# RWKV-7 recurrence and squared-ReLU feed-forward: the third channel tile of the first layer filled with zero rows from 64 to 128

## The chip, the cores and the metric

The kernel runs on one core of a Trainium2 chip. The metric is the device time of one execution in microseconds (us). In the profile PE is TensorE's matmul side and PEld its weight-load side, DVE is VectorE, ACT is ScalarE, POOL is GpSimd and SP is SyncE.

## The reference

For each of 4 batches and 8 heads a 40x40 state runs over 768 time steps. Its outputs of all heads form 3072 tokens of 320 channels, which go through a feed-forward network with 2048 hidden units:

```
for t in range(S):
    y[:, :, t] = einsum('bhd,bhde->bhe', rt, state)
    Sa = einsum('bhde,bhe->bhd', state, at)
    state = state * wt[:, :, None, :] - einsum('bhd,bhe->bhde', Sa, bt) + einsum('bhd,bhe->bhde', vt, kt)
x = y.transpose(0, 2, 1, 3).reshape(3072, 320)
h = maximum(x @ w_in, 0)        # w_in: 320 x 2048
out = (h * h) @ w_out           # w_out: 2048 x 320
```

## The kernel before

The recurrence is computed in chunks of 128 time steps: 6 chunks for each of 4 batches, 24 in all, in the order chunk 0 of all batches, chunk 1 of all batches, and so on. For each chunk `decay` and `rest` transpose the inputs, form running products of the decays and the products of keys with keys by head; `inverse` builds the inverse of a triangular 128x128 matrix for every head, in 6 levels of three stages (a transposition, a product that leaves PSUM through a mask, a product that is added); `chain` does what depends on the state. Heads lie in pairs, 64 partitions each, of which 40 hold data. So most matmuls contract over 128 rows, and those of `products` (the tiles `aT,bT`, `aT,kT`, `rT,vT`, `rT,xnT`) over 40 rows, one parity of heads on partitions 0 to 39 and the other on 64 to 103.

`gather` turns the outputs of two chunks into a tile `tokens`, 256 tokens by channel. The 320 channels are cut into three channel tiles, `KT`: rows 0 to 127, 128 to 255, and 256 to 319, the third with 64 rows only. `w_in` lies in SBUF in the same three channel tiles. For each of 16 hidden tiles (`f`) the first layer makes three matmuls into one PSUM bank, one for each channel tile; this is called an f step below. ACT then takes the ReLU (L395) and DVE the square (L396). The second layer contracts over the 16 hidden tiles, 128 rows each (`w_out,hid`). There are 12 pairs of chunks, hence 12 x 16 = 192 f steps. A float32 matmul of this program is two weight loads and two matmul instructions in the profile, so an f step has six of each: four over 128 rows, two over 64.

The engines take the work in the order in which the generators at the end of the kernel yield it: between two stages of `inverse` or `decay` of the next chunk stand a stage of the present chunk's `chain`, one of `rest`, and up to one part of the feed-forward network of earlier chunks (`second`). A scheduler in the framework may then reorder instructions of one engine.

`mm`, at L65, is the helper that records nearly all matmuls, so they share that line; they are told apart by their tiles (`out<-moving, stationary` or the reverse: the program's names of what is read and written).

Of the kernel before, what the change touches and what calls it, by code (L numbers as in the profile page):

```python
# [17 lines left out]
def kernel(  # L18
# [9 lines left out]
    moe_w_out: bass.AP,  # L28
    out: bass.AP,
):  # L30
    # The recurrence runs in chunks of C steps.  Within a chunk, with E_j the product of the decays
    # of the steps before j and all products taken relative to the middle of the chunk:
    #   a' = a E_t, k' = k / E_t+1, b' = b / E_t+1           (per key channel)
    #   N = strictly lower (a' b'^T), A = strictly lower (a' k'^T)
    #   x = (I + N)^-1 (a' S^T + A v)                         (the rows S a of all steps)
    #   y = E_t (r S + low(r v^T) k' - low(r x^T) b')
    #   S <- E_C (S + v^T k' - x^T b')
    # (I + N)^-1 is exact: the inverses of its diagonal blocks, doubled in size level by level.
    # Heads go in pairs, 64 partitions or columns each; tiles by head are [., parity, pair, .].
    nc = tc.nc  # L40
    B, H, S, D = r.shape
    DM = H * D
# [29 lines left out]
    pair = lambda t_, q: t_[:, 2 * q:2 * q + 2, :].rearrange("t h d -> t (h d)")  # L72
    over4 = lambda m_: m_.unsqueeze(1).to_broadcast([128, NP, 128])

# [1 line left out]
    class Ring:  # L76
        def __init__(self, name, n, shape, fill, pads):
            self.tiles = [single(f"{name}{i}", shape) for i in range(n)]
# [17 lines left out]
    def load(i):  # L96
        bb, c = order[i]
        loaded[i] = {}
        for nm, ring in rings.items():
# [2 lines left out]

    load(0)

# [1 line left out]
    ident = single("ident", [128, 128])  # L106
    make_identity(nc, ident)
    ones = single("ones", [128, MID])
# [2 lines left out]
    nc.gpsimd.memset(upper, 1.0)  # L111
    nc.gpsimd.affine_select(out=upper, in_=upper, compare_op=Alu.is_gt, fill=0.0, base=0,
                            pattern=[[1, 128]], channel_multiplier=-1)
    # -1 at [2p, 2p + 1]: the first level, transposed.
    first = single("first", [128, 128])
    nc.gpsimd.memset(first, 0.0)
    odd = first.rearrange("s (p e) -> s p e", e=2)[:, :, 1]
    nc.gpsimd.memset(odd, -1.0)
    nc.gpsimd.affine_select(out=odd, in_=odd, compare_op=Alu.is_equal, fill=0.0, base=0,
                            pattern=[[-2, 64]], channel_multiplier=1)  # L120
    # -1 where the row is in the second and the column in the first half of one block of 2 n.
    halves = {}
    for lv in range(1, LEVELS):
        n = 1 << lv
# [6 lines left out]
                                pattern=[[-2 * n, count], [0, n]], channel_multiplier=1)  # L131
        nc.gpsimd.affine_select(out=left, in_=left, compare_op=Alu.is_ge, fill=0.0, base=2 * n - 1,
                                pattern=[[2 * n, count], [0, n]], channel_multiplier=-1)
    # 1 where a state's row and column belong to the same head of a pair.
    same = single("same", [128, NP, 2])
    nc.gpsimd.memset(same, 0.0)
    for e in range(2):
# [4 lines left out]
    states = Ring("state", B, [128, NP, 2, DP], 0.0, lambda t_: t_)  # L142

    w_in = single("w_in", [128, len(KT), DFF])
    w_out = single("w_out", [128, NF, DM])

    # Weights come as float64 in raw words: the chip rounds them to float32.  hi holds the sign, 11 bits
    # of exponent and 20 of mantissa, lo the 32 bits below.  With p = sign and power of two, from hi:
    # weight = (p with hi's mantissa) + p lo 2^-52, the sum rounded once.
    def rounded(dst, src, n):  # L150
        raw = work.tile([128, WP, 2], I32, tag="raw", name="raw")[:n, :dst.shape[-1]]
        nc.scalar.dma_start(out=raw.rearrange("p f e -> p (f e)"), in_=src.bitcast(I32))
# [26 lines left out]
            else:  # L179
                rounded(dst, src, rows)  # L180

# [1 line left out]
    def turn(x_):  # L183
        p_ = psum(ps_w)
        for q in range(NP):
# [1 line left out]
        return quads(p_)  # L187

    def products(name, bufs, l_, r_):
        """Strictly upper part of l_^T r_ by head, as one tile a parity."""  # L190
        res = []
        for e in range(2):
            p_ = quads(psum(ps_w))
            rows = slice(e * DP, e * DP + D)
            for q in range(NP):
                mm(p_[:, q], l_[rows, q, :], r_[rows, q, :], True)
            t_ = work.tile([128, NP, 128], FP32, tag=name, name=name, bufs=bufs)
            nc.vector.tensor_tensor(t_, p_, over4(upper), Alu.mult)  # L198
            res.append(t_)
        return res  # L200

    def inverse(g):
        """(I + N)^-1 transposed, from N transposed: both parities in step, a stage at a time."""
        new = lambda nm, bufs: work.tile([128, NP, 128], FP32, tag=nm, name=nm, bufs=bufs)
        both = range(2)
        ns = g["N"]
        tts, ts = [new("inv_t", 4) for _ in both], [new("inv", 2) for _ in both]
        for e in both:
            nc.vector.tensor_tensor(tts[e], ns[e], over4(first), Alu.mult)
            nc.vector.tensor_tensor(tts[e], tts[e], over4(ident), Alu.add)  # L210
        yield
        for lv in range(1, LEVELS):
            src, dst = (tts, ts) if lv == 1 else (ts, tts)
            for e in both:
                p_ = quads(psum(ps_w))
                for q in range(NP):
                    nc.tensor.transpose(p_[:, q], src[e][:, q], ident)  # L217
                nc.scalar.copy(dst[e], p_)  # L218
            yield
            gs = []  # L220
            for e in both:
                p_ = quads(psum(ps_w))
                for q in range(NP):
                    mm(p_[:, q], ns[e][:, q], ts[e][:, q], True)
                gs.append(new("inv_g", 2))
                nc.vector.tensor_tensor(gs[e], p_, over4(halves[lv]), Alu.mult)  # L226
            yield
            last = lv == LEVELS - 1
            for e in both:
                p_ = quads(psum(ps_w))  # L230
                for q in range(NP):
                    if last:
                        mm(p_[:, q], gs[e][:, q], tts[e][:, q], True)
                    else:
                        mm(p_[:, q], tts[e][:, q], gs[e][:, q], True)
                to = tts[e] if last else ts[e]
                nc.vector.tensor_tensor(to, p_, to, Alu.add)  # L237
            yield
        g["TT"] = tts
# [1 line left out]
    turned = lambda nm, bufs: work.tile([128, NP, 128], FP32, tag=nm, name=nm, bufs=bufs)  # L241

    def decay(i, g):
        """Products of the decays, and N, which the inverse waits for."""
        x_ = loaded[i]
        dec = g["dec"] = decays.next()
        up, down = dec[:, 0], dec[:, 1]
        wT = turn(x_["w"])
        for q in range(NP):
            nc.vector.tensor_tensor_scan(up[:, q, MID + 1:C + 1], wT[:, q, MID:], ones, 1.0, Alu.mult, Alu.mult)  # L250
            nc.vector.tensor_tensor_scan(down[:, q, MID - 1::-1], wT[:, q, MID - 1::-1], ones, 1.0, Alu.mult, Alu.mult)
        yield
        nc.vector.reciprocal(down[:, :, MID + 1:C + 1], up[:, :, MID + 1:C + 1])
        nc.vector.reciprocal(up[:, :, :MID], down[:, :, :MID])
        yield
        bT, aT = turned("bT", 1), turned("aT", 2)
        nc.vector.tensor_tensor(bT, turn(x_["b"]), down[:, :, 1:C + 1], Alu.mult)
        nc.vector.tensor_tensor(aT, turn(x_["a"]), up[:, :, :C], Alu.mult)  # L258
        yield
        g["N"] = products("N", 2, bT, aT)  # L260
        g["aT"] = aT
        yield

    def rest(i, g):
        """What the chain needs beside the inverse."""
        x_ = loaded.pop(i)
        up, down, aT = g["dec"][:, 0], g["dec"][:, 1], g["aT"]
        kT, rT, vT = turned("kT", 1), turned("rT", 2), turned("vT", 1)
        nc.vector.tensor_tensor(kT, turn(x_["k"]), down[:, :, 1:C + 1], Alu.mult)
        yield  # L270
        g["A"] = products("A", 4, kT, aT)
        yield
        nc.scalar.copy(rT, turn(x_["r"]))
        nc.scalar.copy(vT, turn(x_["v"]))
        g["rT"] = rT
        yield
        g["RV"] = products("RV", 4, vT, rT)
        yield

        def back(d_):  # L280
            p_ = psum(ps_w)
            for q in range(NP):
                nc.tensor.transpose(p_[:, q * 128:(q + 1) * 128], d_[:, q], ident)  # L283
            return p_.rearrange("t (h d) -> t h d", h=H)[:, :, :D]

        wn = g["wn"] = work.tile([128, H, D], FP32, tag="wn", name="wn")
        nc.scalar.copy(wn, back(up[:, :, :C]))
        yield
        inv = back(down[:, :, 1:C + 1])
        for nm in ("k", "b"):  # L290
            nc.vector.tensor_tensor(x_[nm][:, :, :D], inv, x_[nm][:, :, :D], Alu.mult)
            g[nm] = x_[nm]
        g["v"] = x_["v"]
        yield

# [1 line left out]
    ended, tokens = {}, {}  # L297

    def chain(i, g):
# [63 lines left out]
        gather(i, ys.rearrange("t h d -> t (h d)"))  # L363
        yield

# [1 line left out]
    def gather(i, ys):  # L367
        """Tokens of GB chunks by channel, for the second part."""
        n = i % GB
        if n == 0:  # L370
            tokens[i // GB] = work.tile([128, len(KT), GB * C], FP32, tag="tokens", name="tokens")
        t_ = tokens[i // GB]
        p_ = psum(ps_c)
        for j, (o, m_) in enumerate(KT):
# [9 lines left out]
    def ffn():  # L384
        for gi in range(len(order) // GB):
# [3 lines left out]
            hid = []  # L389
            for f in range(NF):  # L390
                p_ = psum(ps_f)[:, :GB * C]
                for j, (_, m_) in enumerate(KT):
                    mm(p_, w_in[:m_, j, f * 128:(f + 1) * 128], t_[:m_, j, :], j == 0)
                h_ = work.tile([128, GB * C], FP32, tag="hid", name="hid", bufs=NF + 2)
                nc.scalar.activation(h_, p_, Act.Relu)  # L395
                nc.vector.tensor_tensor(h_, h_, h_, Alu.mult)  # L396
# [12 lines left out]
                nc.sync.dma_start(out=out[at:at + C, :], in_=o_)  # L409
                yield True  # L410

    # ---- in the order that the engines take it: while one stage's result leaves PSUM, the tensor
# [1 line left out]
    second = ffn()  # L414
    gathered = set()
    PER_CHUNK = -(-(NF + 4 * GB) // GB)
# [68 lines left out]
```

## Time and profile before

| What | Value |
|---|---|
| Median of 3 runs | 1795.6 us (1790.55 to 1799.59) |
| Span of the profiled execution, first to last instruction | 1795.3 us |
| Mean granted TensorE clock | 0.970 |
| PE busy | 1734.9 us (97%) |
| PEld busy | 1509.1 us (84%) |
| DVE busy | 976.8 us (54%) |
| ACT busy | 335.0 us (19%) |
| POOL busy | 12.2 us (1%) |

The profiled execution has no time of its own beside its span; its span lies 0.3 us under the median of the three runs. Matmuls are pipelined and their ends are modelled, so the durations of single PE instructions overlap; the distance from one start to the next tells what one costs. A row of the timeline gives the start, the length from there to the last end, the engine, line and operation, the tiles, the shape (contraction rows * stationary columns, then the moving operand) and the number of instructions that were merged; in square brackets stands the idle time of the engine before the row and what ended it. "issue" is idle time for which the profile shows no awaited event.

### The profile page before, as it was taken

To read this page: it belongs to the slowest core of one execution; us is meant where nothing else is said; L and a number is where in the kernel's file an instruction comes from. 1 tells how busy PE (TensorE), PEld (TensorE's weight loads), DVE (VectorE), ACT (ScalarE), POOL (GpSimd) and SP (SyncE) were. 2 spreads that over 40 slices of the span, in tenths; PEclk is the share of its full clock that TensorE was granted. 3 is DMA by queue.
4 is the path that set the end of the run, shared out by engine and by line. 5 is a ranking of instruction groups with operands and counts; after the bars stand their busy time and mean duration, and the time that the engine had idled before them with its cause. 6 is when DMAs were issued, how large, how long until landed. Compare 5 with 4: busy or idle time off the path is not lost.

```text
span 1795.3 us, 29170 instructions
## 1 busy us (share of the span) xinstructions
PE 1734.9 (97%) x12408; PEld 1509.1 (84%) x12408; DVE 976.8 (54%) x1921; ACT 335.0 (19%) x717; POOL 12.2 (1%) x61
## 2 busy tenths in 40 slices
PE   4886999999999999999999999999999999999999
PEld 4776888888888888888888888888888888888875
DVE  7989866355455554545645545635635544545411
ACT  0111222112112112212212212212212211211211
POOL 2000000000000000000000000000000000000000
PEclk9868899999999999999999999999999999989999
DMA  7213110010110100100101101001001011000000
GB/s 107 57 50 81 52 23 12 16 26 5 19 23 12 19 20 12 23 16 16 23 12 20 23 12 19 12 16 26 12 16 26 9 19 23 5 1 8 1 8 8
DMA packets 158593, 39.88 MB, mean 22 GB/s; under 512 B 150784, under 2 KB 153856, under 8 KB 158464
## 3 DMA queue, kind: packets, MB, share of 16 engines
q1 hardware_dynamic: 153216, 27.54, 8.9%
q10 hardware_dynamic: 5248, 10.49, 2.0%
q8 instruction: 98, 1.61, 0.4%
q14 instruction: 31, 0.25, 0.0%
HBM read 34.08 MB, written 3.93 MB: 21 GB/s over the span
## 4 chain that ended last, share of the span: by engine, by line
PE 92%; DVE 6%; DMA 2%; issue 0%; ACT 0%; DVEq 0%; ACTq 0%
PE ps_w L65 37%; PE ps_f L65 28%; PE ps_c L65 13%; PE ps_w L217 7%; PE ps_w L186 4%; DMA raw<-in_moe_w_in_dram 1%; PE ps_w L283 1%; PE ps_c L338 1%; PE ps_c L327 1%; PE ps_c L375 1%; DVE power L165 1%; DVE signed L161 0%; DVE inv L237 0%; DVE inv_g L226 0%; DMA raw<-in_moe_w_out_dram 0%; DVE w_in L163 0%
## 5 line engine op out<-in xcount | busy, mean ns | idle before, releaser
L226 DVE TENSOR_TENSOR inv_g<-ps_w,half 128x512 f32<-128x512 f32 x288 | 198.9, 691 | 272.8 <-PE ps_w L65 272.6
L65 PE MATMUL ps_f<-tokens,w_in 128*128 128x256 f32 (+1 forms) x1152 | 323.3, 400 | 0.0
L65 PE MATMUL ps_w<-inv,N 128*128 128x128 f32 x2304 | 298.3, 285 | 0.0
L65 PEld LDWEIGHTS ps_w<-inv,N 128*128 128x128 f32 x2304 | 282.5, 200 | 8.4 <-issue 4.7
L65 PEld LDWEIGHTS ps_f<-tokens,w_in 128*128 128x128 f32 (+1 forms) x1152 | 187.0, 189 | 79.2 <-issue 69.2
L65 PE MATMUL ps_w<-inv_g,inv_t 128*128 128x128 f32 x1920 | 242.0, 279 | 4.8 <-DVE inv_g L226 4.7
L65 PEld LDWEIGHTS ps_w<-inv_g,inv_t 128*128 128x128 f32 x1920 | 228.4, 193 | 19.8 <-issue 12.0
L237 DVE TENSOR_TENSOR inv<-ps_w,inv 128x512 f32<-128x512 f32 x240 | 165.5, 690 | 123.4 <-PE ps_w L65 120.4
L65 PE MATMUL ps_f<-w_out,hid 128*128 128x320 f32 x768 | 220.5, 433 | 0.0
L218 ACT COPY inv_t<-ps_w 128x512 f32<-128x512 f32 x240 | 130.4, 588 | 387.8 <-PE ps_w L217 378.4
L396 DVE TENSOR_TENSOR hid<-hid 128x256 f32<-128x256 f32 x192 | 81.4, 424 | 217.3 <-ACT hid L395 217.3
L65 PEld LDWEIGHTS ps_f<-w_out,hid 128*128 128x128 f32 x768 | 139.6, 190 | 48.5 <-issue 0.7
L395 ACT ACTIVATE hid<-ps_f 128x256 f32<-128x256 f32 x192 | 73.8, 384 | 388.5 <-PE ps_f L65 388.5
L217 PE MATMUL ps_w<-ident,inv 128*128 128x128 f32 x960 | 131.6, 278 | 8.0 <-DVE inv L237 7.8
L217 PEld LDWEIGHTS ps_w<-ident,inv 128*128 128x128 f32 x960 | 106.3, 141 | 37.4 <-issue 13.9
L65 PE MATMUL ps_w<-aT,bT 40*128 40x128 f32 x384 | 43.2, 299 | 25.7 <-DVE aT L258 25.7
L65 PEld LDWEIGHTS ps_w<-aT,bT 40*128 40x128 f32 x384 | 41.8, 205 | 27.9 <-DVE aT L258 26.4
L361 DVE TENSOR_TENSOR ys<-ps_c,wn 128x320 f32<-128x320 f32 x24 | 11.8, 492 | 82.9 <-PE ps_c L65 82.9
L65 PE MATMUL ps_c<-in_b,RX 128*128 128x40 f32 x384 | 52.7, 300 | 1.2 <-DVE RX L198 1.1
L65 PEld LDWEIGHTS ps_c<-in_b,RX 128*128 128x128 f32 x384 | 51.0, 212 | 2.3 <-DVE RX L198 2.2
L65 PEld LDWEIGHTS ps_w<-inv_t,inv_g 128*128 128x128 f32 x384 | 45.6, 192 | 6.3 <-issue 4.4
L237 DVE TENSOR_TENSOR inv_t<-ps_w,inv_t 128x512 f32<-128x512 f32 x48 | 33.2, 691 | 32.1 <-PE ps_w L65 32.1
(115 smaller groups left out, 1802.8 us busy)
## 6 DMA issues: line engine op xcount, KB each, us to landing
raw<-in_moe_w_out_dram ACTq DMA_DIRECT2D x16, 320.0 KB, 2.9
raw<-in_moe_w_in_dram ACTq DMA_DIRECT2D x16, 256.0 KB, 2.7
in_w<-in_w_dram SPq DMA_DIRECT2D x24, 160.0 KB, 2.7
in_a<-in_a_dram SPq DMA_DIRECT2D x24, 160.0 KB, 2.7
in_k<-in_k_dram SPq DMA_DIRECT2D x24, 160.0 KB, 2.7
in_b<-in_b_dram SPq DMA_DIRECT2D x24, 160.0 KB, 3.1
in_r<-in_r_dram SPq DMA_DIRECT2D x24, 160.0 KB, 3.4
in_v<-in_v_dram SPq DMA_DIRECT2D x24, 160.0 KB, 2.7
```

The costliest lines, as they stand in the source:

```text
L65: nc.tensor.matmul(o, l_, r_, start=start, stop=True, skip_group_check=True)
L165: nc.vector.scalar_tensor_tensor(rest, lo, 2.0 ** -52, p_.bitcast(FP32), Alu.mult, Alu.mult)
L186: nc.tensor.transpose(p_[:, q * 128:(q + 1) * 128], pair(x_, q), ident)
L217: nc.tensor.transpose(p_[:, q], src[e][:, q], ident)
L218: nc.scalar.copy(dst[e], p_)
L226: nc.vector.tensor_tensor(gs[e], p_, over4(halves[lv]), Alu.mult)
L237: nc.vector.tensor_tensor(to, p_, to, Alu.add)
L283: nc.tensor.transpose(p_[:, q * 128:(q + 1) * 128], d_[:, q], ident)
L327: nc.tensor.transpose(p_[:, q * 128:(q + 1) * 128], st[:, q].rearrange("p e d -> p (e d)"), ident)
L338: nc.tensor.transpose(p_[:, q * 128:(q + 1) * 128], pair(xn, q), ident)
L395: nc.scalar.activation(h_, p_, Act.Relu)
L396: nc.vector.tensor_tensor(h_, h_, h_, Alu.mult)
```

## The change

The third channel tile is filled with zero rows to 128. `w_in` already had 128 partitions for it; rows 64 to 127 of that part are now set to zero once. The `tokens` tile is no longer drawn from a rotating pool of two buffers but is one of two fixed tiles, used in turn, whose rows 64 to 127 of the third channel tile are set to zero once. The three matmuls of an f step then read all 128 partitions in every channel tile.

```diff
     w_in = single("w_in", [128, len(KT), DFF])
+
+    tails = [(j, m_) for j, (_, m_) in enumerate(KT) if m_ < 128]
+    token_tiles = [single(f"tokens{i}", [128, len(KT), GB * C]) for i in range(2)]
+    for j, m_ in tails:
+        nc.gpsimd.memset(w_in[m_:, j, :], 0.0)
+        for t_ in token_tiles:
+            nc.gpsimd.memset(t_[m_:, j, :], 0.0)
     w_out = single("w_out", [128, NF, DM])
...
         if n == 0:
-            tokens[i // GB] = work.tile([128, len(KT), GB * C], FP32, tag="tokens", name="tokens")
+            tokens[i // GB] = token_tiles[i // GB % 2]
...
                 p_ = psum(ps_f)[:, :GB * C]
-                for j, (_, m_) in enumerate(KT):
-                    mm(p_, w_in[:m_, j, f * 128:(f + 1) * 128], t_[:m_, j, :], j == 0)
+                for j in range(len(KT)):
+                    mm(p_, w_in[:, j, f * 128:(f + 1) * 128], t_[:, j, :], j == 0)
```

Comments are dropped as well, with empty lines in their place. Line numbers from L145 on move up by 7 (L217 becomes L224).

The sequence of instructions on PE, DVE, ACT and SP is the same in both programs, save for line numbers and buffer names. What differs is three instructions more on POOL and where PE asks for POOL's semaphore. At the end of POOL's list stood before:

```order
L138 MEMSET same 64x4 x2
L81 MEMSET minus_x_159 128x8x24
L81 MEMSET state_162 128x512
L81 MEMSET state_163 128x512
L81 MEMSET state_164 128x512
L81 MEMSET state_165 128x512
```

and now:

```order
L81 MEMSET state_162 128x512
L81 MEMSET state_163 128x512
L81 MEMSET state_164 128x512
L81 MEMSET state_165 128x512
L149 MEMSET w_in 64x2048
L151 MEMSET tokens_171 64x256
L151 MEMSET tokens_172 64x256
```

The three new fills stand behind everything that POOL did before.

On PE, at the first f steps (here one row of an f step is one matmul; a shape is that of the moving operand's or output's 128 partitions, not of the contraction) stood before:

```order
L65 MATMUL ps_f<-tokens,w_in 128x256
L65 MATMUL ps_w<-inv_g,inv_t 128x128 [waits DVE_49]
L65 MATMUL ps_w<-inv_g,inv_t 128x128 x3
L65 MATMUL ps_f<-tokens,w_in 128x256 x4
L65 MATMUL ps_f<-tokens,w_in 128x256 [waits Activation_49]
```

and now:

```order
L65 MATMUL ps_f<-tokens_171,w_in 128x256
L65 MATMUL ps_w<-inv_g,inv_t 128x128 [waits DVE_49]
L65 MATMUL ps_w<-inv_g,inv_t 128x128 x3
L65 MATMUL ps_f<-tokens_171,w_in 128x256 [waits Pool_49]
L65 MATMUL ps_f<-tokens_171,w_in 128x256 x3
L65 MATMUL ps_f<-tokens_171,w_in 128x256 [waits Activation_49]
```

The first matmul of a third channel tile now asks whether POOL's fills are done; no instruction has another place.

## The prediction

> **What bounds the kernel now.** I read the page first: the busy shares and the chain of work that ended last.
>
> ```profile
> span 1795.3 us, 29170 instructions
> ...
> PE 1734.9 (97%) x12408; PEld 1509.1 (84%) x12408; DVE 976.8 (54%) x1921; ACT 335.0 (19%) x717; POOL 12.2 (1%) x61
> ...
> PE 92%; DVE 6%; DMA 2%; issue 0%; ACT 0%; DVEq 0%; ACTq 0%
> ```
>
> TensorE carries 92% of the chain. The next view is the busy time by stretch (columns: stretch, length, busy time of PE, PEld, DVE, ACT, POOL with instruction counts, granted clock, DMA share, GB/s), and then who PE waited for (total, times, longest).
>
> ```profile
> 0.00:400.00 400.00, 342.75 (x2407) 308.47 (x2408) 287.45 (x684) 63.07 (x126) 12.25 (x61) 0.89 0.23 48
> 420.00:1510.00 1090.00, 1090.00 (x8087) 950.34 (x8085) 568.62 (x1024) 214.94 (x463) 0.00 (x0) 1.00 0.09 17
> 1510.00:1796.00 286.00, 282.13 (x1772) 232.89 (x1770) 110.78 (x198) 51.76 (x117) 0.00 (x0) 0.96 0.02 6
> ```
>
> ```profile
> PE ps_w L65 <- DVE aT L258: 25.7, 3, 12.5
> PE ps_w L217 <- DVE inv L237: 7.8, 9, 2.3
> ```
>
> From 420 to 1510 us PE is never idle, DVE is busy 52% and ACT 20%. So PE's own sequence sets the time there, and what matters is how far apart its instructions start. PE's visible waits are some tens of us; the largest is three waits for DVE `aT`.
>
> Third, the f step itself: when it first and last starts (the row for its tile), and its groups by shape.
>
> ```profile
> L65 PE MATMUL ps_f<-tokens,w_in x1152: 376/379/483, 205.3 to 1774.3; 128*128 128x256 f32 x192
> ```
>
> ```profile
> L65 PE MATMUL ps_f<-tokens,w_in 128*128 128x256 f32 x768 | 204.1, 387 | 0.0
> L65 PE MATMUL ps_f<-tokens,w_in 64*128 64x256 f32 x384 | 133.6, 428 | 0.0
> L65 PEld LDWEIGHTS ps_f<-tokens,w_in 128*128 128x128 f32 x768 | 130.5, 191 | 16.9 <-issue 7.3
> L65 PEld LDWEIGHTS ps_f<-tokens,w_in 64*128 64x128 f32 x384 | 56.5, 184 | 62.3 <-issue 61.9
> ```
>
> 384 instructions over 64 rows cover 133.6 us (348 ns each), 768 over 128 rows 204.1 us (266 ns each), at the same 256 columns. The weight loads over 64 rows have 62.3 us of idle time before them, 61.9 of it while nothing was awaited: 0.32 us in each of 192 steps. The weight-load timeline near the end, where f steps follow one another, shows both sides of it; the last row is PE's, the second layer's stream.
>
> ```profile
> 1771.26 0.73 PEld L65 LDWEIGHTS ps_f<-tokens,w_in 128*128 128x128 f32 x4 [0.33 <-issue]
> 1772.32 0.29 PEld L65 LDWEIGHTS ps_f<-tokens,w_in 64*128 64x128 f32 x2 [0.33 <-issue]
> 1772.95 0.73 PEld L65 LDWEIGHTS ps_f<-tokens,w_in 128*128 128x128 f32 x4 [0.33 <-issue]
> ...
> 1774.63 17.49 PE L65 MATMUL ps_f<-w_out,hid 128*128 128x320 f32 x64
> ```
>
> Going from 128 rows to 64 and going back each cost a 0.33 us hole in the weight loads. One f step takes 1772.95 - 1771.26 = 1.69 us. What an instruction over 128 rows costs in a stream without a switch comes from the second layer, whose last instruction is 433 ns long by its group:
>
> ```profile
> L65 PE MATMUL ps_f<-w_out,hid 128*128 128x320 f32 x768 | 220.5, 433 | 0.0
> ```
>
> (17.49 - 0.43)/63 = 0.271 us for 320 columns, so 0.217 for 256, and 1.30 us for six of them: 0.39 less than 1.69.
>
> **The change part by part.** *The two matmul instructions over 64 rows become two over 128.* The weight load is 184 ns over 64 rows and 191 over 128; 7 ns x 384 would be 2.7 us, but a load lies beside a matmul that takes 0.217 us, so I take 0. Streaming is by columns in every row shown, 256 before and after; I take 0 for it too. From below nothing is to be had here, since the columns stay.
>
> *The holes.* In the middle of the kernel f steps stand between stages of the inverse. PE's timeline there, and at a place where no f step is near:
>
> ```profile
> 846.10 1.66 PE L65 MATMUL ps_f<-tokens,w_in 128*128 128x256 f32 x6
> 847.69 1.09 PE L217 MATMUL ps_w<-ident,inv 128*128 128x128 f32 x8
> 848.62 1.95 PE L65 MATMUL ps_w<-inv,N 128*128 128x128 f32 x16
> 850.40 1.66 PE L65 MATMUL ps_f<-tokens,w_in 128*128 128x256 f32 x6
> 851.99 2.05 PE L65 MATMUL ps_w<-inv_g,inv_t 128*128 128x128 f32 x16
> 853.88 1.66 PE L65 MATMUL ps_f<-tokens,w_in 128*128 128x256 f32 x6
> ...
> 900.82 1.04 PE L217 MATMUL ps_w<-ident,inv 128*128 128x128 f32 x8
> 901.69 2.32 PE L65 MATMUL ps_f<-w_out,hid 128*128 128x320 f32 x8
> 903.85 1.95 PE L65 MATMUL ps_w<-inv,N 128*128 128x128 f32 x16
> 905.78 2.02 PE L65 MATMUL ps_w<-inv_g,inv_t 128*128 128x128 f32 x16
> ```
>
> The f step takes 1.59 us to the next start (846.10 to 847.69, 850.40 to 851.99), 0.29 over 1.30. The block behind it pays the rest of the way back: `ident,inv` x8 takes 0.93 us there and 0.87 behind a second-layer block (900.82 to 901.69), `inv_g` x16 takes 1.89 (851.99 to 853.88) where 16 such instructions with no switch take 1.78 (848.62 to 850.40). So an f step loses 0.29 + 0.06 to 0.29 + 0.11, that is 0.35 to 0.40 us; near the end it was 0.39. Transpositions follow in about half of the steps, and I take 0.36, nearer to them.
>
> *How many.* Counted along PE's timeline, 23 of the 192 steps are followed by a product over 40 rows, as here (PE, then PEld):
>
> ```profile
> 871.07 1.74 PE L65 MATMUL ps_f<-tokens,w_in 128*128 128x256 f32 x6
> 872.64 1.61 PE L65 MATMUL ps_w<-aT,bT 40*128 40x128 f32 x16
> ...
> 872.10 0.29 PEld L65 LDWEIGHTS ps_f<-tokens,w_in 64*128 64x128 f32 x2 [0.33 <-issue]
> 872.43 1.63 PEld L65 LDWEIGHTS ps_w<-aT,bT 40*128 40x128 f32 x16
> ...
> 879.51 0.63 PEld L65 LDWEIGHTS ps_w<-rT,xnT 40*128 40x128 f32 x5 [0.17 <-issue]
> ```
>
> From 64 rows to 40 there is no hole, and from 128 to 40 there is one (the last row; shorter, since a 128-column transposition stands before it). With the tail at 128 rows the way in will stand before the 40-row product instead, so these steps gain between 0 and half of 0.39 us each, 4.5 us in all; I take 0, by the last row. [...]
>
> Sum: 169 x 0.36 = 61 us. No f step stands before 205 us, and behind that PE's waits are few, so I let it all count, less 1 us for small waits behind a faster PE: 60.
>
> *The fills on POOL.* The nearest rows are the state fills, POOL's last work before (timeline and group):
>
> ```profile
> 11.05 1.92 POOL L81 MEMSET state<- 128x512 f32 x4
> ```
>
> ```profile
> L81 POOL MEMSET state<- 128x512 f32 x4 | 1.9, 533 | 0.0
> ```
>
> At 533 ns for 512 elements a partition, 2048 + 2 x 256 take 2.7 us, from 13.0 to 15.7 us. PE asks for them at 205 us, so that wait is met 189 us early. POOL has nothing behind them. Cost 0; at worst 2.7 us, if DVE's weight conversion were held up for all of it; at best 0, since a fill that was not there cannot give time back.
>
> *The fixed token tiles.* There were two buffers, there are two; the order of the engines is unchanged. Cost 0. The cover for this is that two pairs of chunks lie between uses of one buffer, some 4 x 1795/24 = 300 us at this pace.
>
> **The rivals.**
>
> *(a) DVE or ACT becomes late.* The loop product, DVE eviction, next product now has 0.3 us less beside it where an f step stands in it. Against it: at 903.85 to 905.78 the 16 products run straight into the stage that needs their eviction, with no f step between, and take 1.93 us instead of 1.78. So a stage with no cover at all loses 0.15 us, and an f step of 1.30 us remains as cover. If every gaining step gave back 0.15, it would be 169 x 0.15 = 25 us: 1761 us.
>
> *(b) The clock is halved more often* (the side on which it ends slower). The windows with a halved clock, and the long one without:
>
> ```profile
> 165.60:196.30 30.70, 20.61 (x101) 18.76 (x102) 27.17 (x66) 1.84 (x5) 0.00 (x0) 0.50 0.24 64
> 401.10:1517.30 1116.20, 1116.20 (x8292) 973.53 (x8290) 582.39 (x1047) 221.69 (x478) 0.00 (x0) 1.00 0.09 17
> 1517.30:1527.50 10.20, 10.20 (x51) 9.86 (x51) 3.26 (x5) 0.79 (x3) 0.00 (x0) 0.50 0.11 20
> ```
>
> In a halved window of 10.2 us PE starts 51 instructions, half the usual number, so such a window costs 5.1 us. [...] Between 401 and 1517 us, some 15 chunks at 1795/24 = 75 us, nothing was halved; soon after that it was. If all of those 15 came to be halved, it would cost 77 us and the kernel would take 1735 + 77 = 1812 us; the gain is gone from 12 more halvings on. With 3 more it is 1750, with two fewer 1725. [...]
>
> *(c) The holes are not due to the rows*, but to the third matmul of a group or to the bank. Then nothing changes: 1795. Against it: the same hole stands before the first load over 128 rows of the next step, the 64 instructions of the second layer that share a bank have none, and 64 to 40 rows has none.
>
> **How the numbers follow.** 1795.3 - 60 = 1735 us, and the 0.3 us to the median changes nothing. Chances: the forecast with the clock within three halvings either way 0.84; (a) or a bad clock with part of the gain left, 1752 to 1786 us, 0.08; a better outcome under 1720 us (all 192 steps at 0.39 are 75 us, 1720) 0.03; (c) 0.03; (b) to the end 0.02. The range runs from 1720 (the largest price, or the late halvings gone) to 1752 (the smallest price with three more halvings); it leaves out about 0.16. A measurement of this kernel tells some 0.5% (9 us, the spread of its three runs) from no change: faster 0.95, same 0.03, slower 0.02.
>
> **What would show it.** In the profile after, all 1152 loads and matmuls of `tokens,w_in` have 128 rows, the 61.9 us of idle time before them are down to what a stream over 128 rows has, an f step before `ident,inv` takes 1.30 instead of 1.59 us, near the end 1.30 instead of 1.69; `aT,bT` behind an f step gets a hole of about 0.33 us. PE stays at 97% or more, and the clock from 401 us on tells (b): under 0.97 there means more halvings. Wrong would be holes that stay, or new PE waits for DVE between f steps.

## The result and the profile after

The changed kernel took 1732.3 us (median of 4 runs, 1725.9 to 1735.4), beside 1794.7 us before on the same chip (median of 4). The ratio is 0.9646, with a 95% interval of 0.9617 to 0.9676: 3.5% faster. The forecast was 1735 us. The profiled execution is the fastest of the four.

The page of the changed kernel, as shown of the one before (span, busy time, the chain that ended last):

```profile
span 1724.2 us, 29173 instructions
...
PE 1658.5 (96%) x12408; PEld 1521.9 (88%) x12408; DVE 974.2 (57%) x1921; ACT 334.6 (19%) x717; POOL 14.7 (1%) x64
...
PE 91%; DVE 6%; DMA 2%; issue 0%; ACT 0%; DVEq 0%; ACTq 0%
```

PE's shares of the span and of the chain are within a point of where they were (97% and 92%); 76 us of its busy time are gone at the same 12408 matmuls, and the weight loads, which lost no work, fill 88% of the span instead of 84%. The first layer's groups by shape show where:

```profile
L65 PE MATMUL ps_f<-tokens,w_in 128*128 128x256 f32 x1152 | 282.3, 382 | 0.0
L65 PEld LDWEIGHTS ps_f<-tokens,w_in 128*128 128x128 f32 x1152 | 204.7, 191 | 20.3
```

One shape instead of two. Before, the two groups had 204.1 + 133.6 = 337.7 us of matmul time; now it is 282.3. The 61.9 us of idle time before 64-row loads, for which nothing was awaited, are gone: the 20.3 us left are short gaps, spread over 1152 loads, for which the view names no cause.

PE's timeline in the middle of the kernel, then the weight loads at an f step before a 40-row product:

```profile
816.97 1.46 PE L65 MATMUL ps_f<-tokens,w_in 128*128 128x256 f32 x6
818.27 1.95 PE L65 MATMUL ps_w<-inv_g,inv_t 128*128 128x128 f32 x16
820.05 1.46 PE L65 MATMUL ps_f<-tokens,w_in 128*128 128x256 f32 x6
821.35 1.04 PE L224 MATMUL ps_w<-ident,inv 128*128 128x128 f32 x8
822.22 1.95 PE L65 MATMUL ps_w<-inv,N 128*128 128x128 f32 x16
```

```profile
842.83 1.17 PEld L65 LDWEIGHTS ps_f<-tokens,w_in 128*128 128x128 f32 x6
844.33 1.52 PEld L65 LDWEIGHTS ps_w<-aT,bT 40*128 40x128 f32 x16 [0.33 <-issue]
```

An f step takes 1.30 us to the next start (1.59 before), the `inv_g` block behind it 1.78 (1.89 before), the `ident,inv` block 0.87 (0.93 before). Where `aT,bT` follows, the hole of 0.33 us now stands before `aT,bT`: it moved and did not go.

The spans hold a second difference: span and mean granted clock of the core, before and after:

```profile
core 0: 1795.3 us, clock 0.970
```

```profile
core 0: 1724.2 us, clock 0.977
```

The clock is either whole or halved in these two profiles: every stretch that they record has 1.00 or 0.50 (after, for one, 0.50 from 383.6 to 390.4 us and 1.00 from 455.3 to 1066.3). So span times mean clock is about what the run would take at the whole clock, if PE set the pace throughout: 1795.3 x 0.970 = 1741 us before and 1724.2 x 0.977 = 1685 us after. By this reading about 56 of the 71 us between these two spans are the change's own and 15 are a clock that was halved less in this execution. Taken as a mean over a set of runs, span times mean clock is steadier than the time: between 1742 and 1744 us for three sets of runs of the kernel before (9, 11 and 13 runs), 1682 and 1680 for two sets of the changed one. The difference, 62 us, is also that of the medians.

### The profile page after: what moved, and what is told of

Same layout as the page of the kernel before. It is cut to its first block, busy times and chain, and to the rows that moved or that the text cites. A ratio compares the mean times of both kernels' runs of the same rounds, so it can differ in the third digit from the quotient of the medians.

```text
span 1724.2 us, 29173 instructions
## 1 busy us (share of the span) xinstructions
PE 1658.5 (96%) x12408; PEld 1521.9 (88%) x12408; DVE 974.2 (57%) x1921; ACT 334.6 (19%) x717; POOL 14.7 (1%) x64
## 4 chain that ended last, share of the span: by engine, by line
PE 91%; DVE 6%; DMA 2%; issue 0%; ACT 0%; DVEq 0%; ACTq 0%
PE ps_w L65 38%; PE ps_f L65 27%; PE ps_c L65 13%; PE ps_w L224 7%; PE ps_w L193 4%; DMA raw<-in_moe_w_in_dram 2%; PE ps_w L290 1%; PE ps_c L345 1%; DVE power L172 1%; PE ps_c L334 1%; PE ps_c L382 1%; DVE signed L168 0%; DVE inv L244 0%; DVE inv_g L233 0%; DMA raw<-in_moe_w_out_dram 0%; DVE w_in L170 0%
## 5 line engine op out<-in xcount | busy, mean ns | idle before, releaser
L65 PE MATMUL ps_w<-inv,N 128*128 128x128 f32 x2304 | 291.1, 281 | 0.0
L65 PEld LDWEIGHTS ps_w<-inv,N 128*128 128x128 f32 x2304 | 277.9, 196 | 5.4 <-issue 0.9
L65 PE MATMUL ps_f<-tokens,w_in 128*128 128x256 f32 x1152 | 282.3, 382 | 0.0
L65 PEld LDWEIGHTS ps_f<-tokens,w_in 128*128 128x128 f32 x1152 | 204.7, 191 | 20.3
L224 PE MATMUL ps_w<-ident,inv 128*128 128x128 f32 x960 | 129.6, 275 | 8.0 <-DVE inv L244 7.9
L224 PEld LDWEIGHTS ps_w<-ident,inv 128*128 128x128 f32 x960 | 109.7, 141 | 27.7 <-DVE inv L244 11.4
```

The lines of the kernel that those rows point to most:

```text
L65: nc.tensor.matmul(o, l_, r_, start=start, stop=True, skip_group_check=True)
```

## The experiments

The theory is that TensorE pays about 0.2 us whenever successive matmuls go from contractions over 128 rows to contractions over 64 or 40, or back: half of the 0.35 to 0.40 us that an f step lost before. One visit to 64 or 40 rows costs two such transitions. Counted along PE's timeline, there are 246 visits before and 77 now. That is 169 fewer, not 192: behind 23 f steps follows a 40-row product, and the visit to that stays.

### The tiles and fills without the rows

```diff
-                for j in range(len(KT)):
-                    mm(p_, w_in[:, j, f * 128:(f + 1) * 128], t_[:, j, :], j == 0)
+                for j, (_, m_) in enumerate(KT):
+                    mm(p_, w_in[:m_, j, f * 128:(f + 1) * 128], t_[:m_, j, :], j == 0)
```

> The fixed token tiles and the three fills stay, but the third matmul of an f step contracts over 64 rows again. Theory (the gain is the two holes at the change between 64 and 128 rows): as before, 1795 us within 5, with 0.33 us before each 64-row load. Rival (fixed tiles, fills or another wait brought part of it): under 1785 us; if they brought all of it, 1733.

Measured: 1795.6 us (10 runs) beside 1797.3 before, ratio 0.9989 (0.9974 to 1.0004). The groups of weight loads read as before:

```profile
L65 PEld LDWEIGHTS ps_f<-tokens,w_in 128*128 128x128 f32 x768 | 130.5, 191 | 16.9 <-issue 7.3
L65 PEld LDWEIGHTS ps_f<-tokens,w_in 64*128 64x128 f32 x384 | 56.5, 184 | 62.3 <-issue 61.9
```

So the row count alone makes the gain; tiles and fills neither give nor take anything that these runs can tell (at most 5 us by the interval).

### Half of the f steps

```diff
+                    m_ = 128 if f % 2 == 0 else m_
```

(in the loop of the experiment above)

> Only every second f step (even f) contracts over 128 rows in its third matmul, the others over 64. Theory: the price is paid once per f step, so half of the 61 us is had: 1764 us, within 8, and 96 holes before 64-row loads are left instead of 192. Rival (most of the gain came from a clock that was halved less often, which sets in or not): near 1795 or near 1733.

Measured: 1769.3 us (4 runs), ratio 0.9838 (0.9811 to 0.9865), so 28 us of the 62. Span times mean clock is 1716 us over the runs: 28 of 62 us again. The weight loads of the first layer, and those of the 40-row product that mostly follows where an f step stands before 40 rows:

```profile
L65 PEld LDWEIGHTS ps_f<-tokens,w_in 128*128 128x128 f32 x960 | 169.6, 193 | 18.8 <-issue 3.3
L65 PEld LDWEIGHTS ps_f<-tokens,w_in 64*128 64x128 f32 x192 | 28.6, 186 | 31.9 <-issue 31.7
L65 PEld LDWEIGHTS ps_w<-aT,bT 40*128 40x128 f32 x384 | 40.3, 204 | 33.9 <-DVE aT L265 27.2 <-issue 6.3 <-DVE end L357 0.3
```

Half of the 64-row loads, and half of the idle time before them (31.7 of 61.9 us). The price is paid by the step. The gain is 45% of the whole, and the neighbours account for it: of the 23 steps that stand before a 40-row product, 19 are even ones, which were changed here, and their holes have moved in front of `aT,bT` (6.3 us of idle time for which nothing was awaited, 19 x 0.33). So 77 visits are gone instead of 169, which is 46%, and 28 us over 77 visits is 0.37 us each, as with all steps changed. By the time alone half of the gain could not be excluded: the interval of the ratio is 24 to 34 us.

### 96 rows instead of 128

```diff
+                    m_ = max(m_, 96)
```

> The third matmul contracts over 96 rows, 32 of them zeros, instead of 128. Theory (what counts is whether the rows are over 64): no holes, 1733 us within 6. Rival (every change of the row count drains TensorE): holes of 0.33 us before and behind the 96-row loads, 1795 us.

Measured: 1741.3 us (4 runs), ratio 0.9681 (0.9647 to 0.9714). The holes are gone, though the row count still changes twice in every f step:

```profile
L65 PEld LDWEIGHTS ps_f<-tokens,w_in 128*128 128x128 f32 x768 | 133.3, 192 | 11.1
L65 PEld LDWEIGHTS ps_f<-tokens,w_in 96*128 96x128 f32 x384 | 73.4, 192 | 9.8
```

So it is not any change of the row count that costs a hole. The time is 9 us over that with 128 rows, in another set of runs (there the kernel before took 1797.3 us, 2.6 more), and more than the expectation allowed. In this profile span times mean clock is 1682.6 us, no more than with 128 rows:

```profile
core 0: 1740.0 us, clock 0.967
```

That left two readings: a cost of its own, or the clock.

### 128 and 96 rows again, on one chip

Both kernels as they were.

> The changed kernel once more, on the same chip as the next three. Theory: 1732 us within 6, span times mean clock 1682 us within 4. If the 9 us between it and the 96-row kernel (1741 us) come from the chip, not from the kernel, it moves toward 1741.

> The 96-row kernel once more. Theory (its instructions cost the same as with 128 rows, and what set it 9 us apart is how often the clock was halved): span times mean clock 1682 us as with 128 rows; its time lies wherever the clock puts it, 1732 to 1745 us. Rival (96 rows cost something of their own): span times mean clock 1690 us or more.

Measured: 1732.8 us with 128 rows (4 runs, ratio 0.967, 0.9649 to 0.969), 1739.1 with 96 (5 runs, ratio 0.971, 0.9685 to 0.9736). Span times mean clock is 1680 us for the first and 1682 for the second, so the instructions cost the same within what can be told. The mean clock over the runs is 0.970 and 0.968, in the earlier pair 0.972 and 0.968. What separates the two kernels is how often the clock is halved; why it should be halved more with 96 rows these runs don't settle. In the two profiles the stretches with a halved clock after 250 us add up to 34 us with 128 rows and to 54 us with 96; at half the clock the 20 us more cost 10, and the two spans are 10.1 us apart (1732.9 and 1743.0). Three of the eight such stretches of the 96-row kernel:

```profile
1409.80:1416.60 6.80, 6.80 (x34) 6.80 (x34) 1.18 (x2) 1.17 (x2) 0.00 (x0) 0.50 0.35 61
1481.50:1488.30 6.80, 6.80 (x35) 6.54 (x34) 2.77 (x4) 0.75 (x3) 0.00 (x0) 0.50 0.14 24
1618.00:1624.80 6.80, 6.80 (x36) 6.54 (x33) 2.77 (x4) 0.61 (x3) 0.00 (x0) 0.50 0.00 0
```

These three are 72 us and twice 68 us apart, about one and two chunks, and hold some 35 matmul instructions in 6.8 us each.

### No zero rows at all

The kernel before, with one line changed:

```diff
-    KT = [(o, min(128, DM - o)) for o in range(0, DM, 128)]
+    KT = [(0, 128), (128, 96), (224, 96)]
```

> The kernel before with its 320 channels cut into 128, 96 and 96 instead of 128, 128 and 64: no zero rows, no fixed tiles, no fills; gather makes 24 more copies of 96x128 on ACT, at some 0.26 us each, beside PE. Theory: 1733 us within 8, no holes in an f step. Rival (zero rows as such, or that every third matmul has the row count of its neighbours): 1795 us; half-way if only one of two changes of row count costs.

Measured: 1726.5 us (4 runs), ratio 0.9611 (0.9584 to 0.9637). Loads of the first layer:

```profile
L65 PEld LDWEIGHTS ps_f<-tokens,w_in 96*128 96x128 f32 x768 | 144.4, 190 | 19.7
L65 PEld LDWEIGHTS ps_f<-tokens,w_in 128*128 128x128 f32 x384 | 60.0, 192 | 1.3
```

No holes: the zeros are only a means of having 96 or 128 rows. Whether this cut is even faster than zero rows, by the 6 us between 1726.5 and 1732.3, was asked again:

> Channels cut into 128, 96 and 96 once more. Theory: span times mean clock 1682 us. Open is whether its mean clock of 0.975, and so 1726.5 us, comes again; if it does, this cut is some 6 us faster than zero rows, if it was luck it lies at 0.971 and 1732 us.

Measured: 1733.9 us (6 runs, 1725.5 to 1742.2), ratio 0.9671 (0.9636 to 0.9706), span times mean clock 1681 us, mean clock 0.970 (1683 us and 0.975 the first time). The 6 us did not come again and were the clock's; the two ways of avoiding 64 rows are the same within what can be told.

### Ones instead of zeros in the tokens

```diff
-            nc.gpsimd.memset(t_[m_:, j, :], 0.0)
+            nc.gpsimd.memset(t_[m_:, j, :], 1.0)
```

> The changed kernel with the extra 64 rows of the token tiles filled with ones instead of zeros (those of w_in stay zero, so the products stay the same). Theory (rows count, not what is in them, and the clock follows the place of its windows): 1732 us within 6, mean clock 0.970 to 0.972 over the runs. [...]

Measured: 1731.5 us (4 runs), ratio 0.965 (0.9624 to 0.9676), span times mean clock 1683 us, mean clock 0.973. What stands in the extra rows of the tokens makes no difference that can be told; those of `w_in` stayed zero here, while the cut into 128, 96 and 96 has data in all rows. That the clock follows the place of its windows was supposed; no run here shows what it follows.

### The 40-row products together

If every visit to 64 or 40 rows costs two transitions, the visits that are left can be made fewer. In `rest` the transpositions of r and v move to the stage of k's, and their product stands right behind that of k:

```diff
         nc.vector.tensor_tensor(kT, turn(x_["k"]), down[:, :, 1:C + 1], Alu.mult)
-        yield
-        g["A"] = products("A", 4, kT, aT)
-        yield
         nc.scalar.copy(rT, turn(x_["r"]))
         nc.scalar.copy(vT, turn(x_["v"]))
         g["rT"] = rT
         yield
+        g["A"] = products("A", 4, kT, aT)
         g["RV"] = products("RV", 4, vT, rT)
         yield
```

> The changed kernel with the products of v and r (RV) made right behind those of a and k (A), one stage of the inverse later than the transpositions of k, r and v, so that 40-row products stand together: 53 visits to 40 rows instead of 77. Theory (each visit costs two holes, some 0.39 us): 24 x 0.39 = 9 us less than the changed kernel, 1723 us. Rival (PE waits for the evictions of four products in a row, or for PSUM): 1732 or more, and new waits of PE for DVE.

> The channels cut into 128, 96 and 96, without zero rows, and the 40-row products together as in the kernel before this one. Theory: 9 us less than 128, 96, 96 alone (1726.5), 1717 us. Rival as there: no gain, with new waits of PE for DVE.

Measured: 1720.6 us (5 runs), ratio 0.9605 (0.9582 to 0.9629), and with the cut of 128, 96, 96 it is 1718.5 us (5 runs), ratio 0.9582 (0.9562 to 0.9602). The first is 12 us under the changed kernel on the same chip, where 9 were expected; span times mean clock falls by 13 and 15 us (1667 and 1666, from 1680 and 1681). The waits of PE for DVE did not grow (30.7 us for `aT`, 7.7 for `inv`, 5.3 for `inv_g` in the first); new are three for ACT of 1.4 us each. PE's timeline, the changed kernel's two visits first, then the one visit that took their place:

```profile
850.91 1.38 PE L65 MATMUL ps_w<-rT,xnT 40*128 40x128 f32 x13
852.02 0.37 PE L65 MATMUL ps_w<-aT,kT 40*128 40x128 f32 x1
...
853.66 2.05 PE L65 MATMUL ps_w<-inv,N 128*128 128x128 f32 x16
...
863.05 1.71 PE L65 MATMUL ps_w<-rT,vT 40*128 40x128 f32 x16
864.69 1.09 PE L224 MATMUL ps_w<-ident,inv 128*128 128x128 f32 x8
```

```profile
780.79 1.38 PE L65 MATMUL ps_w<-rT,xnT 40*128 40x128 f32 x13
781.90 0.37 PE L65 MATMUL ps_w<-aT,kT 40*128 40x128 f32 x1
...
783.22 0.27 PE L65 MATMUL ps_w<-rT,vT 40*128 40x128 f32 x1
783.22 0.27 PE L65 MATMUL ps_w<-aT,kT 40*128 40x128 f32 x1
783.33 0.27 PE L65 MATMUL ps_w<-rT,vT 40*128 40x128 f32 x1
783.34 0.27 PE L65 MATMUL ps_w<-aT,kT 40*128 40x128 f32 x1
...
784.65 2.05 PE L65 MATMUL ps_w<-inv,N 128*128 128x128 f32 x16
```

In the changed kernel `rT,xnT` and `aT,kT` already stand together here: 2.75 us (850.91 to 853.66), and 1.64 for `rT,vT` by itself, together 4.39. The visit with all three takes 3.86 us (780.79 to 784.65), 0.53 less; over 24 chunks that would be 12.7 us. (The way into `rT,vT` stands in the row before it and is not in these sums.) The expectation had 0.39 each. It left out that such a visit has a seam more: the second parity of one product lies on partitions 64 to 103 and the first parity of the next on 0 to 39, and at the seam instructions of both start within 0.01 us of each other. The cut of 128, 96, 96 adds nothing that can be told apart from its clock. Both versions beat the kernel before and the changed one; their medians are the lowest here.

## Why the prediction was right

- *PE's own sequence sets the time*: held. PE waited for DVE, ACT, DMA and POOL nearly as much as before:

```profile
PE ps_w L65 <- DVE aT L265: 30.6, 3, 13.2
PE ps_w L224 <- DVE inv L244: 7.9, 9, 2.4
```

  The three waits for `aT` are 4.9 us longer in this execution and 1.4 us longer in that of the second set; all other sums are within 2 us. No new wait between f steps appeared, so rival (a) did not come about. Of the prediction's signs one was missed by a little: PE is busy for 96% of the span, not 97 or more, as about the same waits now stand in a shorter span.
- *The price of an f step, 0.36 us from rows that gave 0.35 to 0.40*: shown. 0.29 us within the step, 0.06 behind it before a transposition, 0.11 before a product. 62 us of difference over the 169 visits that went is 0.37 us each, and 28 us over the 77 of the second experiment as well. Near the end, where the prediction had 1.69 us, three steps now take 3.88 (1699.75 to 1703.63), 1.29 each.
- *The 23 steps before a 40-row product gain nothing*: shown in the timeline (844.33 above) and in the sums. Before, one block of `aT,bT` loads had a hole of 0.33 us (it stands between the parts of an f step, and the view puts its hole down to DVE `end`); now 20 blocks have one, 6.6 us in all, so 19 holes are new:

```profile
L65 PEld LDWEIGHTS ps_w<-aT,bT 40*128 40x128 f32 x384 | 41.8, 205 | 27.9 <-DVE aT L258 26.4 <-DVE end L350 0.3
L65 PEld LDWEIGHTS ps_w<-aT,bT 40*128 40x128 f32 x384 | 40.3, 204 | 37.9 <-DVE aT L265 31.2 <-issue 6.6
```

  Such idle time before the loads of `rT,xnT` grew from 2.7 to 4.0 us, which is four holes more. Together that is 23. The interval of the measured ratio, 58 to 69 us, reaches by itself to the 69 us of a gain in all steps (192 x 0.36); these rows take 23 steps out of it. That 40 and 64 rows belong together was argued from one row; it is borne out by the loads of `aT,bT`, which got holes only when the step in front went from 64 to 128 rows, and 96 rows beside 128 without a hole show that those two belong together. Holes of 0.33 us stand between 64 and 128 rows, and none between 96 and 128 (9.8 us of idle time before all 384 loads over 96 rows) or between 64 and 40 (872.43 before); what in TensorE makes them no profile here shows. No run here has other row counts than 40, 64, 96 and 128.
- *The fills cost nothing*: nearly. Their rows read

```profile
13.04 1.80 POOL L149 MEMSET w_in<- 64x2048 f32 x1
14.79 0.71 POOL L151 MEMSET tokens<- 64x256 f32 x2
```

  which is 2.5 us against an estimate of 2.7, from 13.04 us on as estimated. DVE reaches its first reciprocal at 20.05 us instead of 19.51; it had also waited 0.4 us longer for a DMA there. The experiment without the rows puts the whole at nothing measurable.
- *The clock*: rival (b) named the right uncertainty. The changed kernel's halvings after 250 us come to 20 us in the first profile and to 34 in that of the second set, beside 41 before; the clock was neither worse nor reliably better. The forecast gave the clock no net effect, and the medians bear it out, though a single profile (71 us) does not; that it came within 3 us of the measured median is in part luck, as the four runs lie 9.5 us apart. One reading there is off: 51 instructions in a halved window of 10.2 us are two thirds of the mean number (8292 in 1116.2 us, 76 in 10.2), not half of it. Its price of 5.1 us stands: for the same instructions the time doubles, 16 of `inv,N` in such a window before take 3.58 us (1521.92 to 1525.50) and not 1.78.
- *Rival (c)*, holes from something else than rows, is excluded: with the tiles and fills in place and only the row count as before all holes are back, and with the row count changed in half of the steps half of them are.

## What to carry to other kernels

Look at the idle time of the weight loads for which nothing is awaited, and group it by contraction rows: in this kernel a visit to 64 or 40 rows among matmuls over 128 costs about 0.37 us for going there and back, more than the 0.217 us that one instruction of 256 columns takes. Give such a matmul 96 or 128 rows (zero rows, or a more even cut such as 128, 96, 96; here that took 2.9 to 3.9% off the time), and put those that must stay small next to each other (here 24 visits fewer and 12 us). Count the visits, not the small matmuls: a 40-row product behind 64 rows had no hole of its own (872.43 before). When two versions differ by less than 1% (six runs of one kernel lie 16.7 us apart here), compare span times mean granted clock as well as the time before looking for a cause in the instructions.

## What was not expected of the hardware

- The time between runs of one kernel is spread by the clock in good part: the changed kernel's four runs lie 9.5 us apart (1725.9 to 1735.4), their span times mean clock 5 us; in the first four runs with 96 rows it is 9.5 and 3 us.
- With 96 rows the same sequence at the same cost ran at a mean clock of 0.968 in both sets (9 runs), with 128 rows at 0.970 and 0.972 (8 runs), which is most of the 6 to 9 us between them. What makes the difference stays open.
- 40-row products on different partitions overlap across two blocks of the program, not only within one: at the seam above two start at 783.22 us, and within the block of `aT,bT` at 872.64 before two start at 873.09. It is the likeliest source of the 3 to 4 us by which the gain passed the 9 us of the holes, though no run takes the overlap alone away.
